# Attention, a silu MLP and a soft mixture of experts on one Trainium2 core: a third PSUM bank for the chunk softmax, pages for one step's transposed pieces, three weight loads in a later step, and another bank order for the last piece

## The chip, the cores and the metric

One core of a Trainium2 chip runs the whole kernel. Times are device microseconds of one execution. The kernel before takes 508.51 us, the median of 3 runs (507.24 to 509.31). The profile shown below is one more execution, of 505.46 us.

## The reference

Three stages follow each other. q, k and v have shape 4 x 8 x 576 x 64; w_in is 512 x 2048, w_out 2048 x 512, phi 512 x 32, w1 8 x 512 x 1024 and w2 8 x 1024 x 512.

```python
def _attn_ref(q, k, v, f):
    scores = scale * np.matmul(q, k.transpose(0, 1, 3, 2))
    cum = np.cumsum(np.log(np.clip(f, 0.0001, 1.0)), axis=-1)
    decay = cum[:, :, :, None] - cum[:, :, None, :]
    scores = np.where(causal, -1000000000.0, scores + decay)
    attn = np.exp(scores - np.max(scores, axis=-1, keepdims=True))
    attn = attn / (np.sum(attn, axis=-1, keepdims=True) + 1e-09)
    return np.matmul(attn, v).astype(np.float32)

def _moe_ref(x, w_in, w_out):            # x: 2304 x 512
    h = x @ w_in
    g = h * (1.0 / (1.0 + np.exp(-h)))
    return (g @ w_out).astype(np.float32)

def _moe2_ref(x, phi, w1, w2):           # x: 2304 x 512
    logits = x @ phi                     # 32 slots
    d = np.exp(logits - logits.max(0, keepdims=True))
    d /= d.sum(0, keepdims=True) + 1e-09
    slot_input = (d.T @ x).reshape(E, S_per_e, D)
    for e in range(E):
        slot_out[e] = np.maximum(slot_input[e] @ w1[e], 0.0) @ w2[e]
    c = np.exp(logits - logits.max(1, keepdims=True))
    c /= c.sum(1, keepdims=True) + 1e-09
    return (c @ slot_out.reshape(n_slots, D)).astype(np.float32)
```

## The kernel before

**The steps.** Attention runs first, until about 184 us. Its output x, 2304 tokens, lies in nine chunks of 256 tokens. The MLP then goes in 36 steps, each one chunk and one quarter of d_ff (a *piece*, 256 tokens by 512 features): steps 0 to 15 take chunks 0 to 3, steps 16 to 35 take chunks 4 to 8, four steps each. Step 35 is the last piece. For the two halves of 128 tokens of a piece, PE multiplies x with the weights split into two parts (L619 to L621, `h_part`), ACT takes the tanh of the half (L636) and DVE multiplies (L645); the result `gt` takes a page of a common pool. A half has a PSUM bank of the ring `h`. The product with w_out is folded into phi and into the slots: only g and `g @ (w_out @ phi)` are needed.

**What a finished piece becomes.** The logits need g with features on the partitions. DVE transposes it in blocks of 32 (`blocks`, `gb`, L698), SP writes the blocks to HBM in four DMAs of 128 KB (`park`, `far`, L708), and one DMA of 512 KB reads them back rearranged (`placed`, `gr`, L716). The matmuls `lp` (L726) then sum the four pieces of a chunk to its logits. `gb` lies either in an own page of the pool (steps that `OWN` lists) or in one of two shared buffers; pieces in own pages are written in `square` of the next step, the others in `halfway` of the next step, and from step 24 on at once. Pieces of the last chunk are transposed on PE instead.

**The softmax of a chunk.** `chunk_soft` broadcasts the logits into a PSUM bank `sl` (L803), takes the maximum (L804) and the exponential (L809, ACT), and copies the logits beside it (L811, DVE). `chunk_tr` transposes both into a bank `etp` (L829). `chunk_w` reads the weights of the slots out of it (L838 for the first four chunks, L840 for the others) and, for the softmax over the slots, L851 and L852, whose difference goes to the exponential of L853. `chunk_acc` multiplies the weights with g into a bank `pp` (L863), which DVE adds up (L870). All these banks are of the ring `g`. Two chunks go through this together in steps 19 and 20 (chunks 0 and 1) and in steps 23 and 24 (chunks 2 and 3); later it is one chunk at a time.

**Banks.** `bank(ring)` gives the next bank of a ring, in turn; an instruction that writes a bank waits until the last reader of what was in it is done. From step 16 on the ring `g` is "b5", from step 32 on "b4"; the ring `h` is "014" and, from step 32 on, "01". The last piece is computed with features on the partitions (`h_turned`, `hT`, L658 to L660), in four banks in the order that the ring `h` then has, "1304".

**SP's queue.** SP issues nearly all DMAs in program order. At the end of a step, `ROOM` says how many weight pages (`unit`, 512 KB: eight of w_out by w_out folded, L448, then 32 of w1, L454, and 32 of w2, L456) may have been loaded by then, if pages are free. The tail multiplies them: h (L935) with w1, so (L997) with w2; then o (L979) and the output.

Of the kernel before, what the change touches and what calls it, by code (L numbers as in the profile page):

```python
# [23 lines left out]
NJ = 4  # L24
# [3 lines left out]
EARLY = [(0, 0), (1, 0), (0, 1), (1, 1)]  # L28
AWAY = EARLY + [(0, 2), (1, 2), (0, 3), (1, 3), (2, 0), (2, 1), (2, 2), (3, 0), (3, 1), (3, 2), (2, 3), (3, 3)]
AWAY += [(c, fg) for c in range(4, 7) for fg in range(4)] + [(7, 0), (7, 1), (7, 2)]  # L30
OWN = (14, 15, 16, 17, 21)
SPARSE = (16, 32)
SOON = (12, 24)
AHEAD = ((5, 1), (7, 0), (9, 1), (11, 0), (13, 2), (19, 1), (21, 2))
CAPS = ((0, 12), (5, 6))
LAG = 1
ROOM = ((14, 1), (15, 2), (20, 3), (21, 5), (22, 7), (23, 8), (24, 9), (25, 10), (26, 13), (27, 15), (28, 18), (32, 24), (33, 29), (34, 35), (35, 42), (36, 45))
PARTS = ((0, 256, {}), (256, 128, {0: 1, 3: 2, 5: 2, 7: 2}), (384, 128, {1: 3, 3: 2, 5: 2, 7: 1}))
RING_A, RING_B, RING_T = "014", "235", "b"

# [2 lines left out]
def tile_attention_moe_softmoe(ctx: ExitStack, tc: tile.TileContext, qk, vr, f, wcat, phi, w1, w2, out):  # L43
# [19 lines left out]
    RINGS = {"s": "0123", "r": "23", "m": "45", "a": RING_A, "b": RING_B, "h": "014", "t": "25", "w": "b", "g": "b", "c": "4b"}  # L63
    turn = dict.fromkeys(RINGS, 0)
# [582 lines left out]
    def h_turned(c, fg, us, d0):  # L647
        xh, xl = XC[c]
        if d0 == 0:
            GR[c, fg] = w0.tile([128, 4, CH], F32, name="gr", tag="t", bufs=2)  # L650
            HT.extend(bank("h", [128, CH], "hT") for _ in us)
        elif us[0] == 0:
            GT[c, fg], GS[c, fg] = page([128, 2, 512], "gt")
        for u in us:
            f = slice(128 * u, 128 * u + 128)
            for d in (d0, d0 + 1):
                w = W[4 * fg + d]
                nc.tensor.matmul(HT[u], lhsT=w[:, 0, f], rhs=xh[:, d], start=(d == 0), stop=False)  # L658
                nc.tensor.matmul(HT[u], lhsT=w[:, 0, f], rhs=xl[:, d], start=False, stop=False)
                nc.tensor.matmul(HT[u], lhsT=w[:, 1, f], rhs=xh[:, d], start=False, stop=(d == 3))  # L660
            if d0:
                g = GR[c, fg][:, u]
                nc.scalar.activation(g, HT[u], AF.Tanh, scale=0.5)
                nc.vector.scalar_tensor_tensor(g, g, 1.0, HT[u], op0=ALU.add, op1=ALU.mult)
        if us[-1] == 3:
            release(*WS[fg][d0:d0 + 2])
            if d0:
                release(*XS[c])
# [24 lines left out]
    def blocks(c, fg, own):  # L693
        if own:
            t, sl = page([128, 4, CH], "gb")
        else:
            t, sl = w0.tile([128, 4, CH], F32, name="gb", tag="t", bufs=2), None
        nc.vector.transpose(t.rearrange("p r (b i) -> p r b i", i=32),  # L698
                            GT[c, fg].rearrange("p t (u r j) -> p r (t u) j", u=4, r=4))
        PARK.append((c, fg, t, sl))  # L700

    def park(own, q=nc.sync):
        for piece in [p for p in PARK if (p[3] is not None) == own]:
            PARK.remove(piece)
            c, fg, t, sl = piece
            far = FAR[c, fg] = hbm.tile([4, 32, 4, 256], F32, name="far", tag="far", bufs=16)
            for a in range(4):
                q.dma_start(out=far[:, :, a].rearrange("i j n -> j i n"), in_=t[32 * a:32 * a + 32])  # L708
            if sl:
                release(sl)  # L710
            yield c, fg
# [66 lines left out]
    def chunk_ls(c):  # L778
        nc.scalar.activation(sm["ls"], LP.pop(c), AF.Copy, scale=2.0 if c < NJ else 1.0)
        read.append(c)  # L780

    def last_wide(us):
        for u in us:
            w = sm["WP"][:, 12 + u]
            at = sm["WP"][:, 4 * u:4 * u + 4] if u < 3 else sm["phi"]
            nc.gpsimd.tensor_copy(at, bass.AP(tensor=w.tensor, offset=w.offset, ap=[list(w.ap[0]), [0, 4], list(w.ap[1])]))  # L786
            WIDE.append(at.rearrange("p a s -> p (a s)"))
# [94 lines left out]
    def ct_page(c):  # L882
        t = page([96, 1024], "ct", F32R)[0]
        CTP.append(t)
        CT.update((c + k, t[:, 256 * k:256 * k + 256]) for k in range(4))
# [185 lines left out]
    with tc.manual_schedule():  # L1071
# [80 lines left out]
        def turn_far(k):  # L1152
            todo = [f for f in AWAY if f not in turned and born.get(f, 99) <= k]
            for f in todo[:([0] + [n for at, n in AHEAD if k >= at])[-1]]:
                turned.append(f)
                blocks(*f, k in OWN)

# [23 lines left out]
        def stacked(k):  # L1181
            was[0] = len(LPS)
            if stage[0] is not None:
                w_prime_c(stage[0])
                stage[0] = None
            if mo["wp"] and mo["wp"][0][0] < k - bool(CQ):
                stage[0] = mo["wp"].pop(0)[1]
                w_prime_b(stage[0])
            open_ = not (SPARSE[0] < k < SPARSE[1] and k % 2)
            while open_ and k <= SPARSE[1] and acc and acc[0][0] < k:  # L1190
                chunk_acc(acc.pop(0)[1])
            for f in sorted(flying, key=lambda f: f[1:]) if open_ else ():
                c, fg = f[1:]
                if f[0] < k:
                    flying.remove(f)
                    g_lp(c, fg)
                if SUMMED.get(c) == 4 and f not in flying:
                    if not soft:
                        chunk_ls(c)
                    soft.append(c)  # L1200
            if k >= (NCH - 1) * 4:
                turns[0] = 2
            turn_next(k + 0.25, True)
            if k > SPARSE[1] and acc and acc[0][0] < k:
                chunk_acc(acc.pop(0)[1])

        def square(k):
# [14 lines left out]
            turn_far(k)  # L1222
            if k < SOON[0] or k == OWN[0] - 1 or k >= SOON[1]:
                for f in park(False, nc.gpsimd if k < SOON[0] else nc.sync):
# [9 lines left out]
        for k, (c, fg) in enumerate(steps):  # L1234
            last = k == len(steps) - 1
            mo["k"] = k
            if k == NJ * 4:
                RINGS.update(t="2", g="b5")
            if k == (NCH - 1) * 4:
                turn["h"] = int(RINGS["h"][turn["h"] % 3] != "0")  # L1240
                RINGS.update(h="01", t="25", g="b4")
            mo["cap"] = [n for at, n in CAPS if k >= at][-1]
            if last:
                RINGS.update(h="1304", g="b", c="a2")
                turn.update(h=-1, c=-1)
                h_turned(c, fg, (0, 1, 2, 3), 0)
                stacked(k)
                square(k)
                h_turned(c, fg, (0, 1), 2)
                stacked(k + 0.5)  # L1250
                chunk_ls(c)
                last_wide((0, 1, 2, 3))
                RINGS["g"], turn["g"] = "b0134", -1
                h_turned(c, fg, (2,), 2)
                last_sums(c, (0, 1))
                h_turned(c, fg, (3,), 2)
                ct_page(0)
                ct_page(4)
                mo["umax"] = 8 * NE + 8
                pump()  # L1260
                break
            if c == NCH - 1:
                h_part(c, fg, 0, 0, 2)
                h_part(c, fg, 1, 0, 2)
                stacked(k)
                square(k)
                h_part(c, fg, 0, 2, 4)
                g_tanh(c, fg, 0)
                g_mul(c, fg, 0)
                h_part(c, fg, 1, 2, 4)  # L1270
            else:
                h_part(c, fg, 0, 0, 4)
                g_tanh(c, fg, 0)
                conv_ops(OPS)
                g_mul(c, fg, 0)
                halfway(k)
                h_part(c, fg, 1, 0, 4)
            if c in (0, 1) and fg == 0:
                split_x(c + 2)
            elif NJ <= c < NCH - 1 and fg == 1:  # L1280
                split_x(c + 1)
            elif (c, fg) == (NJ - 1, 3):
                split_x(NJ)
            g_tanh(c, fg, 1)
            g_mul(c, fg, 1)
            born[c, fg] = k
            if k == 0:
                norm_b(NPAIR - 1)
                norm_x(NPAIR - 1)
            if k == 3:  # L1290
                norm_c(NPAIR - 1)
                release((xpool, "x1"), (nrm, "U1"), (nrm, "R"))
            if c < NCH - 1:
                stacked(k)
                square(k)
                conv_ops(OPS)
            elif fg != 2:
                stacked(k + 0.5)
                if fg == 1:
                    square(k + 0.5)  # L1300
            mo["umax"] = max([0] + [n for at, n in ROOM if k + 1 >= at])
            pump()
# [57 lines left out]
```

## Time and profile before

| what | value |
|---|---|
| runs, median (lowest to highest) | 508.51 us (507.24 to 509.31) |
| the profiled execution, its span | 505.46 us, 503.5 us |
| PE, PEld, DVE, ACT, POOL busy | 96%, 71%, 65%, 52%, 33% of the span |
| DMA traffic | 121.53 MB, mean 241 GB/s |
| step 18 starts, step 24, step 30 ends, step 35 (hT) | 298.0, 343.2, 401.4, 435.7 us |
| h of the tail, so of the tail, end | 459.3, 473.7, 503.5 us |

The span is what the profiler saw of the program, the execution's own time what lies around it too. "PE" are the matmuls, "PEld" the loading of their weights, which runs beside them. "SPq" is a DMA as SP issues it: its transfer lands later. A fp32 matmul has two records or more where the program has one. A wait is put down to whatever ended last.

### The profile page before, as it was taken

The numbers are of one execution on the slowest core, as the hardware profiler recorded it, in microseconds if no ns is written. First come the engines' busy times: TensorE is split into PE (matmuls) and PEld (weight loads), VectorE is DVE, ScalarE is ACT, GpSimd is POOL, SyncE is SP. The second block draws the span as 40 slices with busy tenths as digits, with TensorE's granted clock in tenths as the row PEclk, the third lists the DMA queues.
The fourth block names the chain that finished last, engine by engine and source line by source line (L and its number), as shares of the span: only waits on it lengthen the run. The fifth ranks groups of instructions, "written<-read, shape, count | busy, mean of one in ns | idle before, by whom it ended". The sixth has DMA issues, their size and how long they took to land.

```text
span 503.5 us, 11068 instructions
## 1 busy us (share of the span) xinstructions
PE 482.0 (96%) x4035; PEld 356.0 (71%) x4035; DVE 325.3 (65%) x895; ACT 260.0 (52%) x519; POOL 166.9 (33%) x217
## 2 busy tenths in 40 slices
PE   8899999999999999999999999999999999899994
PEld 4687778877777778787777777675666667665562
DVE  6857667776689648999977775566655533143133
ACT  8788989898898657554343334122312323241022
POOL 9777888888878720012300000000000000022000
PEclk9999999999999999999999999999999999999998
DMA  4726765555753349756758899989979679959997
GB/s 142 229 85 179 202 209 154 163 173 161 207 168 109 93 146 370 259 195 170 196 164 285 254 267 299 340 281 297 281 267 330 216 256 412 410 195 401 408 403 278
DMA packets 56827, 121.53 MB, mean 241 GB/s; under 512 B 9764, under 2 KB 28484, under 8 KB 56772
## 3 DMA queue, kind: packets, MB, share of 16 engines
q1 hardware_dynamic: 55428, 116.62, 70.0%
q0 software_dynamic: 1344, 4.20, 2.9%
q8 instruction: 32, 0.52, 0.4%
q14 instruction: 23, 0.19, 0.1%
HBM read 90.45 MB, written 25.39 MB: 230 GB/s over the span
## 4 chain that ended last, share of the span: by engine, by line
PE 69%; DMA 12%; ACT 5%; DVE 5%; SPq 4%; issue 2%; POOL 2%; DVEq 0%; POOLq 0%; ACTq 0%
PE h L619 10%; PE h L621 10%; PE h L620 10%; PE av L310 7%; PE st L253 4%; PE rs L294 4%; PE mx L207 4%; PE st L255 4%; PE so L997 3%; DMA gr<-far 3%; PE h L935 3%; PE pp L863 3%; DMA far<-gb 2%; DMA QA<-mr 2%; PE lp L726 2%
## 5 line engine op out<-in xcount | busy, mean ns | idle before, releaser
L619 PE MATMUL h<-w,xh 128*128 128x512 f32 x280 | 114.8, 410 | 0.0
L621 PE MATMUL h<-w,xh 128*128 128x512 f32 x280 | 110.5, 395 | 0.0
L620 PE MATMUL h<-w,xl 128*128 128x512 f32 x280 | 110.4, 394 | 0.0
L213 DVE CUSTOM_DVE_ANT_0 junk<-mx,mask 128x64 bf16<-128x64 f32 (+3 forms) x128 | 49.9, 414 | 31.4 <-PE mx L207 30.4
L259 ACT ACTIVATE E<-st 128x256 f32<-128x256 f32 (+4 forms) x160 | 63.3, 431 | 12.2 <-PE st L255 9.8
L619 PEld LDWEIGHTS h<-w,xh 128*128 128x128 f32 x280 | 52.7, 188 | 16.3 <-issue 4.9
L621 PEld LDWEIGHTS h<-w,xh 128*128 128x128 f32 x280 | 52.7, 188 | 12.4
L253 PE MATMUL st<-QA,KA 128*128 128x256 f32 (+2 forms) x192 | 55.9, 302 | 4.9 <-DMA QA<-mr 2.0
L620 PEld LDWEIGHTS h<-w,xl 128*128 128x128 f32 x280 | 52.8, 188 | 10.9
L786 POOL COPY arena<-arena 128x128 f32<-128x128 f32 x4 | 1.1, 292 | 177.0 <-ACT gt L636 160.6
L636 ACT ACTIVATE gt<-h 128x512 f32<-128x512 f32 x38 | 22.6, 596 | 63.4 <-PE h L621 60.5
L645 DVE SCALAR_TENSOR_TENSOR gt<-gt,h 128x512 f32<-128x512 f32 x38 | 25.9, 681 | 43.9 <-ACT gt L636 43.9
L255 PE MATMUL st<-QB,KB 128*128 128x256 f32 (+2 forms) x192 | 51.8, 294 | 0.0
L207 PE MATMUL mx<-KA,QA 127*128 127x64 f32 (+2 forms) x192 | 50.0, 326 | 1.2 <-DVE Mt L213 0.6
L310 PE MATMUL av<-E,VF 128*64 128x320 f32 (+4 forms) x448 | 50.8, 364 | 0.0
L276 POOL TENSOR_SCALAR_AFFINE_SELECT E<-E 128x256 f32<-128x256 f32 (+1 forms) x96 | 41.7, 449 | 24.7 <-ACT E L259 23.4
L185 POOL TENSOR_TENSOR QB<-qk,QA 64x576 fp32r<-64x576 f32 x30 | 42.7, 1426 | 2.3
L183 POOL TENSOR_TENSOR KB<-qk,KB 64x576 fp32r<-64x576 f32 x30 | 42.2, 1426 | 1.7 <-ACT KB L177 0.6
L310 PEld LDWEIGHTS av<-E,VF 128*64 128x64 f32 x448 | 29.6, 137 | 17.7 <-POOL E L276 0.3
L253 PEld LDWEIGHTS st<-QA,KA 128*128 128x128 f32 x192 | 34.7, 181 | 9.8 <-ACT E L259 8.4
L698 DVE STREAM_TRANSPOSE gb<-gt 128x1024 f32<-128x1024 f32 x31 | 37.6, 1229 | 4.7 <-DMA WO<-wb 3.0
L633 ACT ACTIVATE gt<-h 128x512 f32<-128x512 f32 x32 | 18.8, 594 | 35.1 <-PE h L621 34.9
(176 smaller groups left out, 782.3 us busy)
## 6 DMA issues: line engine op xcount, KB each, us to landing
unit<-in_w_dram SPq DMA_DIRECT2D x64, 512.0 KB
raw<-in_w_dram SPq DMA_DIRECT2D x32, 512.0 KB
far<-gb SPq DMA_DIRECT2D x108, 128.0 KB
gr<-far SPq DMA_DIRECT2D x27, 512.0 KB
qk<-in_qk_dram SPq DMA_DIRECT2D x14, 576.0 KB
VF<-in_v_dram SPq DMA_DIRECT2D x16, 320.0 KB
RB<-R SPq DMA_DIRECT2D x32, 144.0 KB
WO<-wb SPq DMA_DIRECT2D x32, 128.0 KB
```

Source lines behind the costliest of these rows:

```text
L183: eng.tensor_tensor(KB.of(p)[0:64, h], src[64:128], KB.of(p)[64:128, h], ALU.subtract)
L185: eng.tensor_tensor(QB.of(p)[64:128, h], src[0:64], QA[p % 3][0:64, h, 64:640], ALU.subtract)
L207: nc.tensor.matmul(t[:, 0:w], lhsT=qa[0:127, h, 128 * blk:128 * blk + 128], rhs=ka[0:127, h, k0:k0 + w], start=True, stop=True)
L213: nc.vector.tensor_tensor_reduce(out=junk[:, 0:w], in0=t[:, 0:w], in1=mask[:, 448 - w:448], scale=1.0, scalar=Mx[p][:, h] if j == 5 else - ...
L253: nc.tensor.matmul(t[0:m, o:o + n], lhsT=ka[:, h, k0:k0 + m], rhs=qa[:, h, 64 + q0:64 + q1], start=True, stop=False)
L255: nc.tensor.matmul(t[0:m, o:o + n], lhsT=kb_[:, h, k0:k0 + m], rhs=qb[:, h, q0:q1], start=False, stop=True)
L259: nc.scalar.activation(e[0:m], t[0:m, 0:o], AF.Exp, scale=0.125)
L276: nc.gpsimd.affine_select(out=e, in_=e, pattern=pattern, compare_op=ALU.is_ge, fill=0.0, base=0, channel_multiplier=-1)
L310: nc.tensor.matmul(AVP[p][x][64 * h:64 * h + 64, o0:o0 + n], lhsT=VF[p % 2][:, kb, h], rhs=E[2 * p + h][kb][:, c:c + n], start=kb == 0, st ...
L619: nc.tensor.matmul(o, lhsT=xh[:, d, tok], rhs=w[:, 0], start=(d == 0), stop=False)
L620: nc.tensor.matmul(o, lhsT=xl[:, d, tok], rhs=w[:, 0], start=False, stop=False)
L621: nc.tensor.matmul(o, lhsT=xh[:, d, tok], rhs=w[:, 1], start=False, stop=(d == 3))
```

## The change

Two tables and two settings of the rings change.

- `OWN`: step 21 leaves and step 22 enters. What is transposed in step 22 takes own pages and is written to HBM in `square` of step 23; what is transposed in step 21 takes the shared buffers and is written in `halfway` of step 22.
- `ROOM`: the entry for step 28 goes, those of 32 to 34 are one or two smaller. Three units that were loaded at the end of step 27 are loaded from the end of step 31 on.
- From step 18 to 31 the ring `g` has three banks, "b52", instead of two.
- At the last step the order of the four banks of hT depends on which of the two banks of the ring `h` was used last: "0314" or "1304", so that the bank used last comes third.

```diff
-OWN = (14, 15, 16, 17, 21)
+OWN = (14, 15, 16, 17, 22)
...
-ROOM = ((14, 1), (15, 2), (20, 3), (21, 5), (22, 7), (23, 8), (24, 9), (25, 10), (26, 13), (27, 15), (28, 18), (32, 24), (33, 29), (34, 35), (35, 42), (36, 45))
+ROOM = ((14, 1), (15, 2), (20, 3), (21, 5), (22, 7), (23, 8), (24, 9), (25, 10), (26, 13), (27, 15), (32, 22), (33, 27), (34, 34), (35, 42), (36, 45))
...
             if k == NJ * 4:
                 RINGS.update(t="2", g="b5")
+            if k == NJ * 4 + 2:
+                RINGS["g"] = "b52"
             if k == (NCH - 1) * 4:
...
             if last:
-                RINGS.update(h="1304", g="b", c="a2")
+                late = RINGS["h"][turn["h"] % 2]
+                RINGS.update(h=("1304", "0314")[int(late)], g="b", c="a2")
                 turn.update(h=-1, c=-1)
```

PE at the end of step 24, where the second of the two chunks is accumulated: `h` are the matmuls of the step, `pp` the products of the slots' weights with g, eight for a chunk; in brackets stands whose work an instruction waits for (PE's own where it is the one that read the bank before).

```order
@@ -1826,6 +1827,7 @@
 L620 MATMUL h<-w,xl 128x512
 L621 MATMUL h<-w,xh 128x512
-L863 MATMUL pp<-gt,arena 32x512 x8
 L863 MATMUL pp<-gt,arena 32x512 [waits DVE_49,PE_49]
+L863 MATMUL pp<-gt,arena 32x512 x7
+L863 MATMUL pp<-gt,arena 32x512 [waits DVE_49]
 L863 MATMUL pp<-gt,arena 32x512 x7
 L726 MATMUL lp<-gr,arena 32x256 [waits DMAHW3_49]
```

The matmuls are the same in the same order; the wait for a bank that PE itself and DVE had read moves from the second chunk's pp to the first chunk's, which now takes the bank of the first etp; the second chunk's pp waits for DVE alone.

SP in steps 21 to 23: `gr<-far` reads a piece back, `far<-gb x8` writes the two pieces of a step, `unit` is a weight load.

```order
@@ -193,10 +193,9 @@
 L448 DMA unit<-WO_3915 128x1024
 L448 DMA unit<-WO_3994 128x1024
-L716 DMA gr<-far 128x1024 x2
-L708 DMA far<-gb 32x4x256 x8
+L708 DMA far<-gb 32x4x256 x8
+L716 DMA gr<-far 128x1024 x2
 L448 DMA unit<-WO_4070 128x1024
-L716 DMA gr<-far 128x1024
-L708 DMA far<-gb 32x4x256 x8
-L716 DMA gr<-far 128x1024
+L716 DMA gr<-far 128x1024 x2
+L708 DMA far<-gb 32x4x256 x8
 L454 DMA unit<-in_w_dram 128x1024
 L716 DMA gr<-far 128x1024
```

The eight writes of step 21's pieces move ahead of two reads, and the eight of step 22's pieces behind one more read.

SP around step 28 in the kernel before, with the same names (`unit` are loads of w1 here, in L454):

```order
L716 DMA gr<-far 128x1024
L708 DMA far<-gb 32x4x256 x4
L454 DMA unit<-in_w_dram 128x1024 x3
L716 DMA gr<-far 128x1024
L708 DMA far<-gb 32x4x256 x4
```

In the change the same queue has no unit there; pieces go out and come back one at a time down to the last read, and then (L456 are loads of w2):

```order
L716 DMA gr<-far 128x1024
L708 DMA far<-gb 32x4x256 x4
L716 DMA gr<-far 128x1024
L454 DMA unit<-in_w_dram 128x1024 x25
L456 DMA unit<-in_w_dram 128x1024 x32
```

The three units that stood ahead of the last three pieces' ways out and back are now in the run behind them, which had 22 units before.

## Rows read from the trace of the kernel before

**Rows 1.** The page: busy time and share of the span, by engine.
```profile
PE 482.0 (96%) x4035; PEld 356.0 (71%) x4035; DVE 325.3 (65%) x895; ACT 260.0 (52%) x519; POOL 166.9 (33%) x217
```

**Rows 2.** Waits of PE, 183 to 503.5 us: total us, times, longest.
```profile
PE hT L658 <- DVE gt L645: 1.4, 1, 1.4
PE pp L863 <- DVE arena L852: 1.3, 1, 1.3
PE etp L829 <- DVE arena L852: 1.0, 2, 0.6
PE lp L726 <- DMA gr<-far: 1.0, 1, 1.0
```

**Rows 3.** Timeline of PE, steps 24 and 32: start, us, instruction, count [idle before].
```profile
350.08 0.64 PE L863 MATMUL pp<-gt,arena 128*32 128x512 f32 x4
...
353.35 1.02 PE L863 MATMUL pp<-gt,arena 128*32 128x512 f32 x5 [1.35 <-DVE arena L852]
...
410.69 1.93 PE L863 MATMUL pp<-gt,arena 128*32 128x512 f32 x16
412.44 1.05 PE L726 MATMUL lp<-gr,arena 128*32 128x256 f32 x16
```

**Rows 4.** Timeline of SP's queue, DVE and ACT, steps 23 and 24.
```profile
342.10 6.08 SPq L708 DMA_DIRECT2D far<-gb  x8
...
345.62 0.42 DVE L811 COPY small<-sl 32x256 f32<-32x256 f32 x1 [1.00 <-ACT small L809]
...
347.00 0.58 ACT L636 ACTIVATE gt<-h 128x512 f32<-128x512 f32 x1
...
349.40 2.59 DVE L698 STREAM_TRANSPOSE gb<-gt 128x1024 f32<-128x1024 f32 x2 [1.39 <-DMA far<-gb]
...
352.48 0.21 DVE L838 TENSOR_SCALAR arena<-etp 128x64 f32<-128x64 f32 x1
```

**Rows 5.** Timeline of SP's queue and PE, steps 28 to 30.
```profile
382.26 0.33 SPq L716 DMA_DIRECT2D gr<-far  x1
...
385.32 1.87 SPq L454 DMA_DIRECT2D unit<-in_w_dram  x3
...
386.44 1.48 PE L726 MATMUL lp<-gr,arena 128*32 128x256 f32 x24
...
399.17 0.64 PE L726 MATMUL lp<-gr,arena 128*32 128x256 f32 x8
400.79 0.42 PE L726 MATMUL lp<-gr,arena 128*32 128x256 f32 x4 [0.98 <-DMA gr<-far]
```

**Rows 6.** Chain that ended last, 388 to 402 us: start, us, what.
```profile
390.12 6.54 DMA far<-gb
...
396.81 3.85 DMA gr<-far
```

**Rows 7.** Timeline of DVE, the end of step 34.
```profile
433.62 0.69 DVE L645 SCALAR_TENSOR_TENSOR gt<-gt,h 128x512 f32<-128x512 f32 x1 [2.21 <-ACT gt L636]
435.00 0.69 DVE L645 SCALAR_TENSOR_TENSOR gt<-gt,h 128x512 f32<-128x512 f32 x1 [0.69 <-ACT gt L636]
```

**Rows 8.** Stretches: us, busy PE, PEld, DVE, ACT, POOL, PEclk, DMA share, GB/s.
```profile
435.70:438.60 2.90, 2.86 (x24) 2.86 (x24) 0.00 (x0) 0.00 (x0) 0.00 (x0) 1.00 1.02 407
440.00:446.00 6.00, 6.00 (x49) 5.08 (x47) 1.44 (x4) 3.00 (x7) 1.01 (x3) 1.00 0.34 137
446.00:453.00 7.00, 6.17 (x45) 3.06 (x42) 4.49 (x13) 2.41 (x7) 1.69 (x3) 1.00 0.72 255
453.00:488.00 35.00, 34.50 (x589) 20.33 (x593) 9.04 (x25) 4.21 (x10) 3.45 (x5) 1.00 1.02 405
488.00:503.50 15.50, 8.62 (x147) 5.57 (x139) 5.56 (x12) 4.18 (x9) 0.00 (x0) 0.89 0.80 298
```

**Rows 9.** Timeline of SP's queue and PE, steps 32 on and the tail.
```profile
408.33 24.37 SPq L454 DMA_DIRECT2D unit<-in_w_dram  x22
...
492.84 1.08 PE L997 MATMUL so<-unit,HM 128*32 128x128 f32 x32
```

## The prediction

> **What bounds the kernel now.** I read the waits of PE from the middle of the program on, then the timeline around each wait on PE and on the engine that ends it, then SP's queue. PE is busy in 96% of the span of 503.5 us [rows 1], so the time can only fall by matmuls that go or by PE's idle time, and the change removes no matmul. In the 320 us after attention PE has only a few waits that the profile can name [rows 2]: before the last piece's hT on a multiply of DVE (1.4 us), before a pp on the softmax's L852 (1.3), twice before an etp on the same line (1.0 together, the longer 0.6) and before an lp on a page that comes back from HBM (1.0). The first three are waits for a PSUM bank that somebody still reads, the fourth for data. They add to 4.7 us, and each stands at a place that the diff touches. So the question is, for each of them, what PE would wait for next.
>
> **The pp of step 24.** The softmax of two chunks takes its banks in the order sl, etp, sl, etp, pp, pp from a ring of two, so the second etp lands in the bank of the first, and the second pp in the bank of the second etp, whose last reader is L852. The first pp begins at 350.08 and the second at 353.35, after an idle time of 1.35 [rows 3]: 3.27 us for a group of sixteen records, where the same group begins at 410.69 and is followed at 412.44 without a wait, 1.75 us. The stall is worth 1.52 us by starts. (The idle column says 1.35. The Trainium skill, Perfetto Trace Analysis, section "Summary: the profiler window per engine type", says that TensorE's reported end is an estimate; by its rule the starts are the better ruler, and the 1.52 against 1.35 in these rows agrees.) With three banks the second pp gets the bank of the second sl, and waits only for its own weights, L838. That line ran at 352.48 [rows 4], and would still hold PE until 352.7, so the bank alone returns 0.65. What made L838 late is DVE's transposes of step 23 (L698, 349.40), which sat idle 1.39 us for the HBM writes of step 22's pieces: both used the two shared buffers. The change puts step 22's pieces into own pages, so this wait goes too, unless step 21's writes, now in the shared buffers, take its place; those stand on SP ahead of two reads, a unit and two more reads that come before 342.10, when step 22's writes began [rows 4]. Then L838 stands 1.39 earlier, at about 351.1, and PE wants it at 351.8. All 1.52 us go, with 0.7 to spare.
>
> **The two etp.** With three banks the second etp needs its data (L811) and no longer L852. In step 24 L811 ended at 346.04 [rows 4], before L852 and before PE came to this etp, so the data was there. Both idle times go: 1.0 us [rows 2].
>
> **The lp of step 30.** It has two halves; the first begins at 399.17, the second at 400.79, 1.62 us later, where sixteen such records took 1.05 busy [rows 3, 5], so some 0.5 for eight: the stall is 1.12 us. The way back shows the cause: three units of 512 KB issued at 385.32 [rows 5], a read of 512 KB, then the four writes of the piece, whose last was issued at 390.12 and landed 6.54 later; the read back took 3.85 and landed at 400.66 [rows 6]. The change takes the three units out of this place. A unit takes 1.3 us in a full queue: 524 KB at 405 GB/s [rows 8] is 1.29. Three of them are 3.9 us of queue; even if half of it only were on the way of this piece, the 1.12 us go. PE itself gets here 2.5 us earlier by the steps above, and so do the transposes that the chain starts from.
>
> **The hT of the last step.** The first hT takes the bank that DVE's last multiply reads from 435.00 to 435.69 [rows 7], and PE sits idle 1.4 us [rows 2]. The change asks which of the two h banks was used last and starts with the other one, read by the multiply of 433.62, done at 434.31, when PE has just become free. The bank of the late multiply comes third: 12 matmuls stand before it, and 24 of them took 2.9 us [rows 8], so it begins some 1.45 us after the first, at 435.8. That is 0.1 later than the release. So 1.4 goes and at most 0.1 comes back.
>
> **What is added.** (1) On SP the read of a piece of step 21 now stands ahead of step 22's eight writes and waits until PE has finished step 23's second half, about 342.6; behind it are those writes, which were issued from 342.10 [rows 4]: half a microsecond, but the eight writes now also hold two pages that step 24's activation needs. That tanh ran at 347.00. Its page comes free when the first four writes have landed. The nearest price is the write of rows 6, 6.54 from issue to landing with 2 MB ahead of it; here only one read of 512 KB is ahead, so I estimate 4 to 5 us after an issue of 343.5, 348.0. The tanh then is late by 2 us against now, yet DVE only comes to its multiply after the transposes, about 349.3, and L838 stands right behind it. Up to a landing of 349.2 PE loses nothing; beyond that it loses one for one. At 6.54 it would be 350.0, a loss of 0.8; as bounds I take nothing and 2 us, and for the sum nothing, since less is queued ahead than in rows 6. (2) The third ring bank is used by nobody else in steps 18 to 31 except the transposes of chunk 8's pieces, and there the second half waits for L852 of step 31, some 4 us done. Nothing. (3) The three units go to the run of 22 behind the last read (408.33, x22) [rows 9], 3.9 us more for DMA engines that are busy 0.34 of 440 to 446 and 0.72 of 446 to 453 [rows 8]: idle for 4.0 and 2.0 us. The tail can take them.
>
> **Sum.** 1.52 + 1.0 + 1.12 + 1.4 = 5.04, less 0.05 to 0.1 at the third hT: 5.0 us. The profiled execution took 505.46 us (span 503.5), so it becomes 500.5. The median of the runs, 508.51, stands 3.05 above the profiled one; I take the same difference off: **503.5 us**.
>
> **Rivals.**
> *Handed back in part.* Either the page of step 24's tanh comes late by up to 2 us, as above, or the lp of step 28 (386.44) becomes the new waiter: its third group reads the page whose read was issued at 382.26 [rows 5] and would by the 3.85 of the read at 396.81 [rows 6] land at 386.1, while it is used at about 387.4. PE arrives 2.5 us earlier; where the transfers don't move with it, 1.2 us are lost. For it: both are margins of about a microsecond. Against: the transfers start from PE's and DVE's own releases, so most of the chain moves along. With 1.2 to 2 us back, some with both, the time is 505 to 507, centre 505.3.
> *It doesn't do what it says.* The waits that the profile puts down to a bank are ended by data a moment later: DVE's transposes still wait for shared buffers, so pp returns 0.65 of 1.52; the hT waits for its third bank instead of its first; the lp's chain is bound by the write and the read back, not by the units. Then 0.65 + 1.0 are left, and the time is 506.9. Against it: the HBM write is named as what held DVE [rows 4], and a write of 128 KB took 6.54 behind the units [rows 6].
> *Slower, by the tail's transfers.* With 25 units in one run the stream has 57 units from about 404.7 on (408.33 less 3.6). At 405 GB/s (1.29 us each), 3.9 for the last landing and all 6 idle us kept, the last lands at 488.1, just after PE wants it: the last group of so begins at 492.84 [rows 9], 487.8 when it comes 5 us earlier. That is break-even, and the point from which it decides: any slower rate costs 57 times the difference. The stretch from 488 to 503.5 has 298 GB/s at a share of 0.80 [rows 8], 372 GB/s while busy, so 1.41 us each: the last unit lands at 495.0, 7.2 late, and the time is 503.5 + 7.2 = 510.7. Against it: the 6 idle us would have to stay although more is queued, and 35 us of the same loads run at 405. (The Trainium skill, DMA: Bandwidth & Descriptors, section "Specifications", puts the HBM limit of a core at about 358 GB/s; by it a unit takes 1.46 us and the case would end near 513.5. The trace disagrees: 405 GB/s over 35 us [rows 8].)
>
> **How the numbers follow.** About 0.5% (2.5 us) is what a measurement here can tell from no change. Forecast 0.58, all of it faster. Handed back 0.25, centred on 505.3, 3.2 below now: 0.14 faster, 0.11 same. Not what it says 0.10: same. Slower tail 0.07: 510.7 is itself 2.2 above, so 0.02 same and 0.05 slower, where the rate is lower still. That gives 0.72 faster, 0.23 same, 0.05 slower. The range runs from 501.5 (the forecast, and the runs' own spread of about 2 us) to 507.2, which takes in the second and the third case; the slower one is left out. The forecast alone spans 501.5 to 504.5.
>
> **What would show it.** Right: PE's waits from 183 us on no longer list hT, pp, etp and lp of these four places; the second pp follows the first by 1.75; DVE's transposes in step 24 begin without idle time; the lp halves of step 30 are 0.5 apart; the third hT waits at most 0.1. Wrong: a tanh in step 24 that waits for HBM writes with a pp behind it, an lp in step 28 that waits for its page, or so and h of the tail waiting for units.

## The result and the profile after

The changed kernel takes **502.63 us** (median of 13 runs, 500.76 to 505.78) where the kernel before takes 508.51 (13 runs): a ratio of 0.9884, with a 95% interval from 0.9858 to 0.9911, or 4.5 to 7.2 us less. The forecast was 503.5.

The profiled executions alone would have misled: that of the change has a span of 502.7 us, only 0.8 below the 503.5 of before. The page of the change:

```profile
span 502.7 us, 11071 instructions
PE 482.6 (96%) x4035; PEld 356.3 (71%) x4035; DVE 325.9 (65%) x895; ACT 259.8 (52%) x519; POOL 166.6 (33%) x217
```

PE does the same work as in [rows 1]. Two things hide the gain. The first lies ahead of everything that the change touches. The first softmax (sl, L803) starts 2.6 us later than before, at 310.25; before it stood at 307.64. Here are the stretches from 20 to 30 us (columns as in [rows 8]), first of the kernel before:

```profile
20.00:25.00 5.00, 4.04 (x28) 3.61 (x28) 3.94 (x19) 3.57 (x9) 3.47 (x5) 1.00 0.94 284
25.00:30.00 5.00, 4.83 (x69) 4.21 (x69) 2.88 (x11) 4.31 (x9) 3.63 (x7) 1.00 0.50 156
```

And of the change:

```profile
20.00:25.00 5.00, 3.98 (x20) 3.64 (x21) 3.13 (x15) 2.75 (x7) 3.10 (x5) 0.75 0.88 272
25.00:30.00 5.00, 4.94 (x40) 4.33 (x42) 3.10 (x13) 4.01 (x8) 3.14 (x6) 0.91 0.56 174
```

The granted clock there is a mean of 0.75 and 0.91 of full speed, so part of these stretches ran at 1.2 instead of 2.4 GHz, in attention; PE was busy for 8.9 of the 10 us in both. Not all of the 2.6 us stand there. The matmul that starts at 20.04 before starts 0.36 later in the change, the one of 28.00 starts 1.51 later, so 1.15 went in between; the rest went before 20 us and, at full clock, between 40 and 184. So I compare from the first sl to the end of the span: 195.9 us before, 192.5 after, 3.4 less. Up to the last o, which leaves out the output behind it, the rows give 188.15 before and 184.68 after, 3.47 less; first of the kernel before, then of the change:

```profile
495.79 1.66 PE L979 MATMUL o<-ct,SO 96*128 96x512 f32 x5 [0.75 <-DVE SO L967]
494.93 1.67 PE L979 MATMUL o<-ct,SO 96*128 96x512 f32 x5 [0.74 <-DVE SO L967]
```

The second thing is in the waits of PE from the first softmax on (columns as in [rows 2]), of the change:

```profile
PE lp L726 <- DMA gr<-far: 0.8, 1, 0.8
PE o L979 <- DVE SO L967: 0.7, 1, 0.7
PE pp L863 <- DVE arena L838: 0.5, 1, 0.5
PE etp L829 <- ACT small L809: 0.4, 1, 0.4
PE etp L829 <- DVE small L811: 0.3, 1, 0.3
```

All four lines of [rows 2] are gone: no hT, no L852, no lp of step 30. The o and the etp on L809 were there before, in the tail. But three new waits stand there, 1.6 us: pp in step 24, now on L838; an etp in step 25 on L811; and an lp that is the one of step 28. The timeline of the change shows what is behind them:

```profile
332.49 1.24 DVE L698 STREAM_TRANSPOSE gb<-gt 128x1024 f32<-128x1024 f32 x1
334.23 1.25 DVE L698 STREAM_TRANSPOSE gb<-gt 128x1024 f32<-128x1024 f32 x1 [0.50 <-DMA far<-gb]
...
345.27 5.31 SPq L708 DMA_DIRECT2D far<-gb  x8
...
350.11 2.37 DVE L698 STREAM_TRANSPOSE gb<-gt 128x1024 f32<-128x1024 f32 x2
...
352.31 0.60 ACT L636 ACTIVATE gt<-h 128x512 f32<-128x512 f32 x1 [3.07 <-DMA far<-gb]
...
353.54 0.22 DVE L838 TENSOR_SCALAR arena<-etp 128x64 f32<-128x64 f32 x1
353.81 1.92 PE L863 MATMUL pp<-gt,arena 128*32 128x512 f32 x16 [0.50 <-DVE arena L838]
...
383.87 0.33 SPq L716 DMA_DIRECT2D gr<-far  x1
...
389.16 0.64 PE L726 MATMUL lp<-gr,arena 128*32 128x256 f32 x8 [0.82 <-DMA gr<-far]
```

The first two lines are the transposes of step 21's pieces, now into the shared buffers: the second waited 0.50 for writes, and PE did not. Those of step 23's pieces (350.11) begin without idle time, as forecast. But ACT sat idle for 3.07 us ahead of the tanh of step 24 until the writes of step 22 had landed, and L838 behind it on DVE came just too late. The read of step 28, issued at 383.87, was used at 389.16: both margins that the prediction named as a rival, in this execution.

### The profile page after: what moved, and what is told of

It reads as the page before. It is cut to its first block, busy times and chain, and to the rows that moved or that the text cites. A ratio compares the mean times of both kernels' runs of the same rounds, so it can differ in the third digit from the quotient of the medians.

```text
span 502.7 us, 11071 instructions
## 1 busy us (share of the span) xinstructions
PE 482.6 (96%) x4035; PEld 356.3 (71%) x4035; DVE 325.9 (65%) x895; ACT 259.8 (52%) x519; POOL 166.6 (33%) x217
## 4 chain that ended last, share of the span: by engine, by line
PE 71%; DMA 10%; ACT 6%; DVE 4%; POOL 4%; issue 2%; SPq 2%; DVEq 0%; POOLq 0%; ACTq 0%
PE h L619 12%; PE h L621 11%; PE h L620 11%; PE av L310 5%; PE st L253 4%; PE mx L207 4%; DMA far<-gb 4%; PE rs L294 3%; PE st L255 3%; PE so L997 3%; PE h L935 3%; PE lp L726 2%; PE pp L863 2%; DMA QA<-mr 2%; ACT KA L177 2%
## 5 line engine op out<-in xcount | busy, mean ns | idle before, releaser
L636 ACT ACTIVATE gt<-h 128x512 f32<-128x512 f32 x38 | 22.7, 596 | 65.8 <-PE h L621 58.9
L207 PEld LDWEIGHTS mx<-KA,QA 127*128 127x128 f32 x192 | 33.4, 192 | 5.3 <-DVE Mt L213 1.8
```

What stands on the lines that cost most here:

```text
L207: nc.tensor.matmul(t[:, 0:w], lhsT=qa[0:127, h, 128 * blk:128 * blk + 128], rhs=ka[0:127, h, k0:k0 + w], start=True, stop=True)
```

## The experiments

In the table, "from sl" is the time from the first sl to the end of the span, in the profiled execution, and "to o" the part of it up to the start of the last o; waits are those of PE, in us, from the first sl on. The ratio is to the kernel before, measured on the same chip. What lies behind the last o differs from one execution to the next, from 7.1 to 8.2 us in all kernels but the last one, while "to o" agrees within 0.05 us where the same waits are gone (the rows with five zeros, 182.60 to 182.65, and 182.71 with five more units in the tail). So differences of less than a microsecond are read from "to o".

| kernel | ratio (95%) | from sl | to o | etp | pp | lp 28 | lp 30 | hT |
|---|---|---|---|---|---|---|---|---|
| before | 1 | 195.9 | 188.15 | 1.0 | 1.35 | 0 | 1.0 | 1.4 |
| the change | 0.9884 (0.9858 to 0.9911) | 192.5 | 184.68 | 0.3 | 0.50 | 0.82 | 0 | 0 |
| ring alone | 0.9977 (0.9953 to 1.0) | 194.7 | 187.45 | 0 | 1.61 | 0 | 1.47 | 1.4 |
| own pages alone | 0.9973 (0.9953 to 0.9994) | 194.7 | 186.98 | 1.0 | 0 | 0 | 1.08 | 1.4 |
| units alone | 0.9984 (0.9967 to 1.0001) | 194.6 | 187.34 | 1.0 | 1.36 | 0.23 | 0 | 1.4 |
| hT order alone | 0.9993 (0.9972 to 1.0014) | 194.6 | 187.50 | 1.0 | 1.31 | 0.28 | 1.33 | 0 |
| the change, again | 0.9884 (0.9848 to 0.9919) | 190.6 | 182.65 | 0 | 0 | 0 | 0 | 0 |
| the change, third time | one run, 501.41 us | 190.3 | 182.60 | 0 | 0 | 0 | 0 | 0 |
| without the units' part | 0.9916 (0.9893 to 0.994) | 191.2 | 183.59 | 0 | 0 | 0 | 0.54 | 0 |
| without the own pages' part | 0.9932 (0.9891 to 0.9974) | 191.8 | 183.58 | 0 | 0.97 | 0 | 0 | 0 |
| one unit at step 24 later | 0.9855 (0.982 to 0.989) | 190.4 | 182.64 | 0 | 0 | 0 | 0 | 0 |
| two units at step 27 later | 0.9896 (0.9858 to 0.9935) | 191.3 | 183.61 | 0.46 | 0.30 | 0 | 0 | 0 |
| both of these | 0.9866 (0.9831 to 0.9901) | 190.1 | 182.61 | 0 | 0 | 0 | 0 | 0 |
| five more units in the tail | 0.997 (0.9937 to 1.0003) | 193.2 | 182.71 | 0 | 0 | 0 | 0 | 0 |

**Each part by itself.** First the ring alone, in the kernel before:

```diff
+            if k == NJ * 4 + 2:
+                RINGS["g"] = "b52"
```

> The kernel before with the third bank (ring b52 from step 18) and nothing else. Theory A (each wait was for the bank): both etp idle times (0.35 and 0.64 us) go; the second pp of step 24 still waits, now for L838, which DVE's transposes hold back by their 1.39 us wait for HBM writes: its idle time falls from 1.35 to about 0.7. Together 1.6 us less, the lp and hT waits stay at 1.0 and 1.4. Theory B (the bank was only the last of several things that came at the same time): the two etp idle for data instead (0.3 and more each) and pp keeps over 1.1; less than 0.6 us in all.

```profile
349.70 2.58 DVE L698 STREAM_TRANSPOSE gb<-gt 128x1024 f32<-128x1024 f32 x2 [1.42 <-DMA far<-gb]
352.77 0.21 DVE L838 TENSOR_SCALAR arena<-etp 128x64 f32<-128x64 f32 x1
353.04 1.92 PE L863 MATMUL pp<-gt,arena 128*32 128x512 f32 x16 [1.61 <-DVE arena L838]
```

These rows of its timeline fit neither theory whole. Both etp waits went, so they were for the bank. But pp waits longer than before, 1.61, on the line that theory A named. Counted from the first sl, which stands 0.73 later in this execution (308.37), PE is ready for the second pp 1.3 us sooner than before (at 351.43 here, 352.00 there), and L838, behind transposes that wait 1.42 for HBM writes, comes only 0.4 us sooner (352.48 in [rows 4]). The lp of step 30 took half a microsecond more, too.

Then the own pages alone:

```diff
-OWN = (14, 15, 16, 17, 21)
+OWN = (14, 15, 16, 17, 22)
```

> The kernel before with step 22 in place of step 21 among the steps whose pieces take own pages, and nothing else. Theory A: DVE's transposes of step 24 begin without idle time (1.39 us before), but the tanh of step 24 now waits for a page until the first four HBM writes of step 22 have landed (about 3 us idle on ACT, as the changed kernel shows), so L852 comes only some 0.5 us sooner: pp's idle time falls from 1.35 to about 0.8. Theory B: the tanh wait is hidden behind the transposes, and pp's idle time falls to about 0. The etp, lp and hT waits stay (1.0, 1.0, 1.4).

```profile
349.16 0.60 ACT L636 ACTIVATE gt<-h 128x512 f32<-128x512 f32 x1 [1.31 <-DMA far<-gb]
350.85 3.64 PE L863 MATMUL pp<-gt,arena 128*32 128x512 f32 x32
```

Theory B: the tanh waits 1.31, it is hidden, and the 32 records of pp run through without a gap. In this kernel, with the old ring, pp lost its wait by the pages alone.

The units alone:

```diff
-... (27, 15), (28, 18), (32, 24), (33, 29), (34, 35), ...
+... (27, 15), (32, 22), (33, 27), (34, 34), ...
```

> The kernel before with the three weight units moved from the end of step 27 to the end of step 31 and beyond, and nothing else. Theory A: the lp wait of step 30 (1.0 us idle) goes, no lp wait comes in step 28 because PE gets there no earlier than before, and the tail shows no wait for a unit: 1.0 to 1.1 us less. Theory B (the way out and back to HBM bounds this lp whatever else is queued): it stays above 0.7 us. Theory C (the tail's transfers become the bound): so L997 waits for units and the time rises.

Theory A for step 30 and for the tail (no wait for a unit). The 0.23 in step 28 came although PE was no earlier: it belongs to this execution, as the next one shows, which has it without any change to the units. The hT order alone:

```diff
-                RINGS.update(h="1304", g="b", c="a2")
+                late = RINGS["h"][turn["h"] % 2]
+                RINGS.update(h=("1304", "0314")[int(late)], g="b", c="a2")
```

> The kernel before with the bank of hT chosen by which h bank was used last, and nothing else. Theory A: the wait of 1.4 us before the first hT goes, the third hT waits at most 0.1: 1.3 to 1.4 us less. Theory B: the third hT waits for the late multiply instead and keeps 0.5 us or more. Everything ahead of step 35 is as before.

Theory A: neither the first nor the third hT waits. Up to the last o the execution is only 0.65 faster, because lp waits of 0.28 and 1.33 stand in it where the kernel before had 0 and 0.98; the 1.3 from sl on are that and a shorter end (7.1 us behind the last o, 7.7 before). The times of its twelve runs show no difference; the interval just reaches the 1.4 us of the wait. Up to the last o the four gains are 0.70, 1.17, 0.81 and 0.65, 3.3 us, where all together are worth 5.5 in the executions below. What is missing went to waits at other places: to pp and lp with the ring alone, to lp in the other three. For the units and the hT order those lp waits are of these executions, since neither edit brings PE to step 28 sooner; so the gap is not shown to come from the parts being alone.

**The change again.** The same kernel in two more executions.

> The changed kernel once more, unaltered. Its first profiled execution had a granted clock of 0.75 in 20 to 25 us and of 0.91 in 25 to 30, and reached the first softmax 2.6 us later than the kernel before. Theory A (that dip is an event of one execution and has nothing to do with the change): where the clock is 1.00 there, the first softmax starts at 307.5 to 308.5 and the span is about 500, by 3.4 us and more below the kernel before; the waits left from step 18 on (pp 0.5, etp 0.3, lp of step 28 0.8) are the same or smaller. Theory B (the change brings it): the dip is there again.

> The changed kernel a third time, for one more profile. Theory A (what was handed back in its first profile, 0.5 for pp, 0.3 for etp and 0.8 for lp of step 28, belongs to executions in which transfers land later, not to the change): from the first softmax to the end 190.6 us with none of these waits, or 192.4 with all of them together. Theory B: a mixture that does not go together, one wait with and one without.

Waits of PE from the first softmax on, in the second execution, all of them:

```profile
PE o L979 <- DVE SO L967: 0.7, 1, 0.7
PE etp L829 <- ACT small L809: 0.4, 1, 0.4
PE si L1050 <- ACT arena L1040: 0.3, 1, 0.3
PE h L935 <- DVE SM L1064: 0.2, 1, 0.2
PE sl L794 <- DVE gr L664: 0.2, 1, 0.2
```

and three rows of its timeline:

```profile
349.69 0.60 ACT L636 ACTIVATE gt<-h 128x512 f32<-128x512 f32 x1 [1.51 <-DMA far<-gb]
...
350.33 3.77 PE L863 MATMUL pp<-gt,arena 128*32 128x512 f32 x32
...
385.26 1.48 PE L726 MATMUL lp<-gr,arena 128*32 128x256 f32 x24
```

190.6 and 190.3 us from sl on: 5.2 and 5.5 less than before, with nothing handed back. Up to the last o (491.83 in the second execution) both are 5.5 less. The tanh still waits for the writes (1.51, and 1.81 the third time), but L838 comes in time. Of the first softmax my expectation was wrong: it started at 309.18 with the clock at 0.73 and 0.93 in the two stretches, and at 309.16 in the third execution with the clock at 1.00 from 20 to 30. So a late start comes without the dip too. Six profiles show one more source, an lp at 285 to 290 us that waited for its page, 0.2 in the third execution and 1.53 in all in "one unit at step 24 later" (first sl at 311.03). The dip is not the change's: of the fourteen profiles eight have it, the units alone and the hT order alone among them, and neither edit touches what runs before 300 us.

**What each margin hangs on.** One unit later at step 24, so that a free page is left for the tanh:

```diff
-... (23, 8), (24, 9), (25, 10), ...
+... (23, 8), (25, 10), ...
```

> The changed kernel without the entry (24, 9) in the table of weight units: one unit is loaded at the end of step 24 instead of step 23, so a free page is left for the tanh of step 24. Theory A (the page that comes back only when HBM writes land is what holds this tanh, and through it pp): ACT has no wait for writes there, the second pp waits 0.1 at most and the etp of step 25 not at all, 0.5 to 0.8 us less than the changed kernel in the profile from step 18 on. Theory B (pp waits for the transposes of DVE in any case): pp keeps 0.4 or more. Below what the times can tell.

```profile
349.91 0.58 ACT L636 ACTIVATE gt<-h 128x512 f32<-128x512 f32 x1
```

The tanh has no wait, as theory A has it, and pp and etp none. Since two executions of the change have none either, this edit buys a margin rather than time. Two units later at step 27:

```diff
-... (26, 13), (27, 15), (32, 22), ...
+... (26, 13), (28, 15), (32, 22), ...
```

> The changed kernel with (28, 15) in place of (27, 15): two units are loaded at the end of step 27 instead of step 26, behind the read of the page that the lp of step 28 waited for. Theory A (that read queues behind the two units): it takes 4 us or less instead of 5.25 and the lp of step 28 has no wait (0.8 before), while the lp of step 30 stays without one: 0.8 us less in the profile. Theory B (the read is late because the writes ahead of it landed late): the wait stays above 0.5.

The lp of step 28 has no wait, as theory A has it, though two executions of the change have none there either; but pp (0.30) and etp (0.46) do, in step with a tanh that waited 2.87: this execution is of the kind of the first one, and its lp was spared. Both edits together:

> Both of the last two edits together in the changed kernel. Theory A: none of the waits for pp, etp and lp of steps 24 to 30 is left, 1.5 us less than the changed kernel from step 18 on in a profile, a ratio of about 0.997 to it. Theory B (the waits only move on): a new wait of PE above 0.5 us appears in steps 25 to 34 or in the tail, and the time is that of the changed kernel.

No wait is left in steps 18 to 34, and no new one came: 190.1 us from sl on. The ratios of 0.9855 (step 24 alone) and 0.9866 (both) stand below the change's 0.9884 of the same runs, but well within each other's intervals. It is the better version if one wants the margins; that it is faster isn't shown.

**Undoing one part of the change.** The units back in step 28:

> The changed kernel with the old table of weight units, so that three units stand in the queue of step 28 again. Theory A (the lp of step 30 is bound by transfers, and takes back what the steps ahead of it gained): its wait is above the 1.0 us of the kernel before, about 1.5 to 2.5, and the whole is 1.5 to 2.5 us slower from the first softmax to the end than the changed kernel's best profile (190.6 us). Theory B (each wait stands for itself): 1.0 us of wait, 1.1 slower.

```profile
399.59 0.64 PE L726 MATMUL lp<-gr,arena 128*32 128x256 f32 x8
400.76 0.64 PE L726 MATMUL lp<-gr,arena 128*32 128x256 f32 x8 [0.54 <-DMA gr<-far]
```

Neither theory: the wait is 0.54, smaller than before, and the whole 0.6 slower than the change at its best, 0.94 up to the last o. The chain of transfers moved up with PE: the read of this page was issued 89.2 us after the first sl before ([rows 6]), and 85.7 us after it here. The same lp waited 0.98, 1.47, 1.08, 1.33 and 0.54 in the five profiles that have the units there: a term of 0.5 to 1.5, and not one of 1.12. The own pages back to step 21:

> The changed kernel with step 21 in place of step 22 among the steps with own pages, as before. Theory A (the third bank alone leaves pp behind DVE's transposes, which wait for HBM writes): the second pp of step 24 waits 1.3 to 1.7 us for L838, all else is gone; 1.4 to 1.8 slower than the changed kernel's best profile from the first softmax to the end (190.6 us). Theory B (as my first reckoning had it, PE's earlier start left out): 0.65 of wait.

```profile
350.96 2.55 DVE L698 STREAM_TRANSPOSE gb<-gt 128x1024 f32<-128x1024 f32 x2 [0.82 <-DMA far<-gb]
354.00 0.21 DVE L838 TENSOR_SCALAR arena<-etp 128x64 f32<-128x64 f32 x1
354.27 1.92 PE L863 MATMUL pp<-gt,arena 128*32 128x512 f32 x16 [0.97 <-DVE arena L838]
```

The mechanism is theory A's, the size between the two: pp waits 0.97 for L838, behind transposes that wait 0.82 for writes. The two parts are not alike: the pages alone free pp, while the ring alone frees the two etp and hands part of that on to pp, whose wait is then 1.61 or 0.97. With both, nothing is left.

**The tail.** Five more units in the run behind the last read:

```diff
-... (25, 10), (26, 13), (27, 15), (32, 22), ...
+... (25, 10), (32, 22), ...
```

> The changed kernel with five more weight units moved into the run that follows the last read (30 instead of 25). Theory A (the tail had 2.6 to 4 us between the landing of the last unit and its use, a unit takes 1.28): 6.4 us more in the queue, less the 1 us that stays idle in 446 to 453, is 1.5 to 3 us more than the tail has; so L997 waits for units and the time is 1.5 to 3 us longer than that of the changed kernel. Theory B (the queue still has room in 440 to 453): no wait for units, no change.

The stretches at the end, of this kernel:

```profile
490.00:495.00 5.00, 2.09 (x13) 1.01 (x11) 2.60 (x5) 1.96 (x5) 0.00 (x0) 1.00 1.00 374
495.00:499.40 4.40, 0.00 (x0) 0.00 (x0) 0.00 (x0) 0.00 (x0) 0.00 (x0) 0.58 1.03 385
```

and of the change, second execution:

```profile
490.00:495.00 5.00, 2.67 (x14) 1.38 (x14) 2.89 (x6) 2.12 (x5) 0.00 (x0) 1.00 0.78 284
495.00:499.40 4.40, 0.00 (x0) 0.00 (x0) 0.00 (x0) 0.00 (x0) 0.00 (x0) 0.70 0.63 233
```

In the profile the size was right (2.5 us), the place was not: PE waits for no unit, and its last o starts at 491.25 against 491.83, 182.71 and 182.65 after the first sl. What is late is the output. Its writes stand behind the units in the queue, the DMA engines are full up to 499.4 us (1.00 and 1.03 against 0.78 and 0.63), and from the last o to the end of the span it is 10.4 us instead of 8.0. The ratio goes back to 0.997. By the ratios that is some 4 us more than the change, more than theory A's 1.5 to 3, though the intervals leave room for 2.5; the profiled execution (503.59 us) is one of the fastest of the ten runs (median 505.34), and no trace shows where the others lost more.

## Why the prediction was right

The time, its sign and its size held: 5.0 us forecast, 5.9 measured (4.5 to 7.2), 5.2 and 5.5 from the first sl on in the two profiles that handed nothing back, 3.4 in the one that did. The terms held too. Counted from the first sl, the same matmuls of PE start earlier in the second execution of the change than before, by 1.28 us at the second etp of step 24 (346.94 before, 347.20 there), 2.71 at the second pp, 3.88 at the second half of the lp of step 30, 5.31 at the first hT and 5.50 at the last o. So the four places gave 1.28, 1.43, 1.17 and 1.43, where the sum had 1.0, 1.52, 1.12 and 1.4.

Two of the signs of being wrong did show in the first execution, though: a tanh in step 24 that waits for writes with a pp behind it, and an lp in step 28 that waits for its page. That execution is the rival "handed back in part", and gave back 2.0 us up to the last o.

- **pp, 1.52.** The wait went, but what it took were the pages: alone they freed pp. The step that failed is "the bank alone returns 0.65": alone it returned nothing there (1.61 of wait instead of 1.35). I set L838 against PE's old arrival, though the same bank brings PE there 1.3 us sooner, and L838 came only 0.4 sooner, behind transposes that wait for HBM writes.
- **The two etp, 1.0.** Right with the ring alone; by starts 1.28, because I took the idle column here and not the starts.
- **The lp of step 30, 1.12.** The wait went, and by starts the term was right in the second execution. It is not a fixed price: undoing it in the finished kernel costs 0.54 of wait, 0.94 us up to the last o.
- **hT, 1.4.** Right. In the second execution DVE's earlier multiply ended at 431.92 and the first hT began at 431.97; the third hT does not wait at all, where I had allowed 0.1.
- **The page of the tanh in step 24.** I estimated that the writes land at 348.0 on the old clock of events, and a limit of 349.2. The etp of step 23 stands at 342.67 before and at 344.80 in the first execution of the change, so its tanh at 352.31 is 350.2 by that clock: 1.0 past the limit, and 0.5 of idle time lost at pp, with 0.3 more at the etp of step 25. In the second one, whose tanh of step 23 was 1.06 later than before, 349.69 is 348.6: within, nothing lost. Place, limit and price held; which side an execution falls on was not to be told from one trace.
- **The lp of step 28.** I reckoned 386.1 for the landing from 3.85 of another read. In the first execution the read needed 5.25 (383.87 to 389.12), and 0.82 was lost of the 1.2 that the rival allowed.
- **The tail.** Three units were absorbed: no wait, and the share in 440 to 446 rose from 0.34 to 1.03 in the first execution and 0.99 in the second. The slower rival needed PE to wait for units; the run with five more showed that the outputs are hit before.
- **The median.** I put the same difference on the median as on the profiled execution. No row supports that: the profile of before lies 3.05 below its kernel's median, the first one of the change 2.2 above. The medians differ by 5.9, more than the profiles of the two kernels do from sl on (5.5 at most), and 5.0 lies within the interval; that the forecast came within 0.9 of the median is in part luck.

What stays open is why transfers land later in some executions than in others, the first one and that of "two units at step 27 later" among them. Each had both a late start of the first softmax and a clock dip; others that had both, the second execution and "both of these", handed nothing back.

## What to carry to other kernels

A wait for a bank is often followed closely by a wait for data, so ask for the next two releasers of the waiting instruction, and set them against the time at which PE will then come, not at which it came. A part that returns little alone can be worth its full wait once the part behind it is done too. And where a kernel's executions differ by some microseconds, compare stretches between two common events, here from the first sl to the last o, in more than one profile, and let the times of many runs say how large the gain is.

## What the hardware showed that I had not expected

The granted clock fell below full speed between 20 and 30 us in eight of fourteen profiles (means of 0.83 to 0.86), of kernels that are the same up to that point. PE was busy for 6.3 to 9.2 of these 10 us where it fell and for 8.0 to 9.1 where it stayed at 1.00, so these rows do not tell what brings it. A ninth profile, "one unit at step 24 later", has the dip at another place: 0.57 from 287 to 291 us, right behind two lp waits of 0.89 and 0.64 and a stretch of 3 us (284 to 287) in which PE was busy for 1.47. And a DMA queue that is too long for the tail did not show as a wait of PE at all: only as 2.5 us more between its last o and the end in the profile.
